# A later due time for one GpSimd clear in the work list of an attention, soft-MoE and MLP kernel

## The chip, the core and the metric

The kernel runs on one core of a Trainium2 chip. The metric is device time in microseconds (us) of one execution, lower is better. The core has five engines that run at the same time and wait for each other through semaphores: TensorE (PE in the profile; its weight loads are PEld), VectorE (DVE), ScalarE (ACT), GpSimd (POOL) and SyncE (SP), which here issues nearly all DMAs.

## The reference

```python
def reference(q, k, v, moe_phi, moe_w1, moe_w2, moe2_w_in, moe2_w_out):
    # attention: B=4, H=8, S=576, D=64, stride 32
    scores = q @ k.T / sqrt(D)
    # heads 0..3: keys of the last 32 positions; heads 4..7: keys at the same position modulo 32
    scores = where(mask, scores, -1e9); attn = softmax(scores); x = attn @ v
    x = x.transpose(0, 2, 1, 3).reshape(2304, 512)
    # soft MoE: 8 experts with 4 slots each
    logits = x @ phi
    slot_in = softmax(logits, axis=0).T @ x
    slot_out[e] = relu(slot_in[e] @ w1[e]) @ w2[e]        # w1: 512x1024, w2: 1024x512, float32
    x = softmax(logits, axis=1) @ slot_out
    # MLP: 512 -> 2048 -> 512 with elu
    h = x @ w_in; g = where(h > 0, h, exp(min(h, 0)) - 1)
    return g @ w_out
```

## The kernel before

The program has three stages. **Attention** (about the first 80 us of the trace) works on 20 units, in the order of the string `ORDER`. A unit marked L is a third of the rows of two heads with the local mask, a unit marked S a quarter of the rows of two heads with the strided mask. The units are numbered here from 0 as `ORDER` has them: 2, 6, 7, 8, 10, 11, 13 and 14 are strided, the others local; units 12 and 15 to 19 are local units of the second pair of heads. A unit goes through these steps: scores on TensorE (L543 local, L562 strided, the latter from a copy of q that GpSimd makes in L551), selection by mask, maximum and subtraction on VectorE (L577 to L605), exponential on ScalarE (L610), sum, reciprocal and transpose on VectorE (L614 to L640; the product with the reciprocal of a strided unit is GpSimd's, L629), a product with the mask on GpSimd for local units (L644, `f_keep`), four copies into a block-diagonal tile (L658 on ScalarE, L660 on GpSimd; "spreads" below), the product with v on TensorE (L671 local, L684 strided), and the move of the result into x by ScalarE (L691 local, L697 strided). The block-diagonal tile `bd` has two halves, which units take in turn, so a unit can spread only when the product of the unit two places ahead in the ring has read its half. Transposes of x (L787, moved out by L799) and the logits (L778) follow the units.

The tiles that hold zeros must be cleared once. Some clears stand in the program text; others (`lv`, `lt`) are nodes of a work list like the steps above. Entry 5 of `lt` is GpSimd's clear of the second half of `bd` (L343), and unit 1 waits for it, as the first that uses that half. Entries 0 to 3 clear a buffer `ex`, two parts of the keys tile `kB` (L304, L305) and a tile `pst`; entry 4 (`late_e0`, L326 to L330) makes a small table `e0`.

The order of every engine's instructions in the attention stage is made by `list_order`, while the program is built: a node is (engine, duration, dependencies, key, function, ring, earliest start). Of the nodes of an engine that could start within `AE` of the earliest one, it takes that with the lowest key, books the planned duration, and goes on. One node's planned start thus moves what is chosen after it, on every engine. On the chip each engine then runs its own list in order.

**The soft MoE** (to about 124 us) takes 8 + 8 weight matrices of 2 MB, which SP loads into regions that attention has finished with; the loads of the first matrices are nodes of the same list (`w_node`), so that SP waits for the unit that used the region last. w1 products are L924, w2 products L1015 and, for the last expert, L1010. Between attention and L924 lies a chain of small steps (L391 to L912). The products on TensorE stand in a fixed order with some filler products in between (`warm`, L314). **The MLP** (the rest) is ordered by a list of its own, which does not contain the attention.

Of the kernel before, what the change touches and what calls it, by code (L numbers as in the profile page):

```python
# [19 lines left out]
def attn_moe_mlp(ctx, tc, q, k, v_l, v_s, phi, w1, w2, w_in, w_out, out):  # L20
# [172 lines left out]
    def small(tag, n, name, bufs, *dims):  # L193
        t = sl_p.tile([128, {"pt": 576, "xt": 768}[tag]], F32, tag=tag, name=name, bufs=bufs)
        t = t[:, 0:n]
        if len(dims) == 2:
            t = t.rearrange("p (a b) -> p a b", b=dims[1])
        elif len(dims) == 3:
            t = t.rearrange("p (a b c) -> p a b c", b=dims[1], c=dims[2])
        return t  # L200
# [56 lines left out]
    with tc.manual_schedule():  # L257
# [80 lines left out]
        def clear(e, t, x):  # L338
            if e == "A":
                return lambda: nc.scalar.activation(out=t[:, x:x + 1024], in_=zero.to_broadcast([128, 1024]), func=AF.Copy)  # L340
            return lambda: nc.gpsimd.memset(t[:, x:x + 1024], 0.0)
# [17 lines left out]
        def load_w(e, second, s, *parts):  # L359
            if (e, second) not in wsl:  # L360
                wsl[e, second] = (w_tile_at(s) if isinstance(s, int) else s)[:, 0:4096]
            t = wsl[e, second]
            for a, b in parts or ((0, 4096),):
                nc.sync.dma_start(out=t[:, a:b], in_=(w2 if second else w1)[e, :, a:b])
# [46 lines left out]
        def emit_acc(t, acc, j0, j1):  # L411
# [7 lines left out]
        anodes, count, apools = [], {}, {  # L419
            "sp": (2, []), "sl": (3, []), "ss": (2, []), "cb": (1, []), "pst": (2, []), "mx": (3, []), "sm": (4, []), "tr": (2, []),  # L420
            "bd": (2, []), "o": (2, []), "qw": (2, []), "t": (3, []), "l": (1, []),
        }
# [6 lines left out]
        def an(eng, dur, deps, key, fn, alloc=None, instr=0):  # L429
            anodes.append((eng, dur, list(deps), key, fn, alloc, 0.0))  # L430
            if instr:
                count[len(anodes) - 1] = instr
            return len(anodes) - 1
# [18 lines left out]
        for x in range(0, WB, 1024):  # L452
            lv[3, x] = an("G", 0.95, [], 14.0 + x / 512, clear("G", v3_sb, x))
        lt = [an("G", d, [], x, f) for d, x, f in zip((0.95, 1.15, 1.15, 0.55, 1.5, 1.8), (12.0, 11.0, 11.1, 13.0, 30.0, 9.5), late)]
        RATE = 2.42
        post = []

        def load_node(kind, p, a, b, after=(), pre=None):
# [4 lines left out]
            key = T[need] - (14 if kind != "v" else 9)  # L463
            dur = 128 * 4 * (b - a) / 1e6 * RATE
            if kind == "v" and p >= 2:
# [27 lines left out]
        def w_node(i, e, s, a, b, after, second=0):  # L493
            post.append((200.0 + i, 128 * 4 * (b - a) / 1e6 * RATE, after, lambda: load_w(e, second, s, (a, b)), None))

# [450 lines left out]
        lt = small("pt", 576, "lt", 2, NSET, 32)  # L946
# [540 lines left out]
```

## Time and profile before

| | before |
|---|---|
| median of 3 runs | 346.62 us (346.04 to 347.05) |
| profiled execution | 346.24 us, of which the trace's span is 344.5 us |
| TensorE busy | 327.6 us, 95% of the span |
| VectorE busy | 262.7 us, 76% |
| ScalarE busy | 250.1 us, 73% |
| GpSimd busy | 62.3 us, 18% |
| DMA | 70.51 MB, mean 205 GB/s |

The shares are means over stages that differ: in the first 150 us the DMA engines are full, in the last 200 us they are nearly idle, and GpSimd works in the attention stage almost alone. A row of a timeline gives the start in us, the length in us, the engine and line, and what it writes and reads; "x" counts instructions that follow each other, and a bracket gives the time for which the engine stood idle before, and what ended it. TensorE's float32 products count as two instructions each.

### The profile page before, as it was taken

The page shows a single profiled execution, that of the slowest core. Times are in us where ns is not written, and L with a number is a line of the kernel's source. Part 1 is how long each engine was busy: PE and PEld are TensorE (multiplying, and loading weights), DVE is VectorE, ACT ScalarE, POOL GpSimd, SP SyncE. Part 2 cuts the span into 40 slices and gives each one's busy share as a digit, 9 for nine tenths or more (in the row PEclk, how much of TensorE's full clock was granted, in tenths as well). Part 3 has the DMA queues.
Part 4 walks back from the last instruction along what each step waited for, and adds up shares of the span by engine and source line. Part 5 has one row for each costly group of instructions (what it writes and reads, how often), then busy time and mean ns, then how long its engine had stood idle before and what let it go on. Part 6 is the DMA issues. An engine that isn't in the chain of part 4 may idle for free.

```text
span 344.5 us, 7046 instructions
## 1 busy us (share of the span) xinstructions
PE 327.6 (95%) x2690; PEld 251.3 (73%) x2690; DVE 262.7 (76%) x586; ACT 250.1 (73%) x498; POOL 62.3 (18%) x106
## 2 busy tenths in 40 slices
PE   4689979999899999999999999999999999999995
PEld 3578866774233345888788888878888888888884
DVE  7899888843713649989999999999975755565862
ACT  9588999985125439999998699668776576657770
POOL 8989525530208300000000000000000000000000
PEclk9699999999999999999999999999999999999999
DMA  7999999999999999693000060000011300110201
GB/s 279 401 416 416 421 417 424 423 409 418 420 431 423 406 416 429 245 434 150 1 0 3 0 243 2 0 0 0 3 62 61 122 2 0 63 61 0 92 33 61
DMA packets 12785, 70.51 MB, mean 205 GB/s; under 512 B 1616, under 2 KB 2640, under 8 KB 8912
## 3 DMA queue, kind: packets, MB, share of 16 engines
q1 hardware_dynamic: 12608, 69.93, 49.9%
q8 instruction: 21, 0.34, 0.4%
q10 hardware_dynamic: 144, 0.13, 0.1%
q14 instruction: 12, 0.10, 0.1%
HBM read 65.34 MB, written 4.72 MB: 203 GB/s over the span
## 4 chain that ended last, share of the span: by engine, by line
PE 75%; DMA 9%; DVE 7%; POOL 4%; ACT 3%; issue 2%; DVEq 0%; SPq 0%; POOLq 0%
PE ops L1362 18%; PE ops L1364 18%; PE ops L1363 18%; PE hps L1300 5%; DMA ex<-in_moe_w_dram 4%; DMA q<-in_moe_w_dram 4%; PE o_ps L671 2%; PE xtps L787 2%; PE s_ps L543 2%; PE ops L1355 1%; ACT bd L658 1%; DVE sc L590 1%; PE mps L1189 1%; PE lg L778 1%; PE so L684 1%
## 5 line engine op out<-in xcount | busy, mean ns | idle before, releaser
L1317 DVE SCALAR_TENSOR_TENSOR g<-hps,g 128x512 f32<-128x512 f32 (+2 forms) x84 | 50.9, 610 | 12.7 <-ACT g L1312 11.7
L1308 ACT ACTIVATE g<-hps 128x512 f32<-128x512 f32 (+2 forms) x84 | 44.8, 534 | 7.9 <-PE hps L1300 7.6
L1312 ACT ACTIVATE g<-g 128x512 f32<-128x512 f32 (+2 forms) x84 | 47.8, 572 | 1.4
L1323 ACT ACTIVATE ghi<-g 128x512 fp32r<-128x512 f32 (+1 forms) x39 | 23.2, 596 | 17.0 <-DVE g L1317 15.0
L1323 ACT ACTIVATE rings<-g 128x512 fp32r<-128x512 f32 (+1 forms) x39 | 22.9, 588 | 17.2 <-DVE g L1317 16.2
L1364 PE MATMUL ops<-w,glo 128*128 128x512 f32 (+1 forms) x87 | 32.8, 377 | 0.0
L1364 PE MATMUL ops<-wh,glo 128*128 128x512 f32 x84 | 31.8, 379 | 0.0
L1300 PE MATMUL hps<-pers 128*128 128x512 f32 (+1 forms) x80 | 29.6, 372 | 0.1
L658 ACT ACTIVATE bd<-tr 32x288 f32<-32x288 f32 (+1 forms) x60 | 28.7, 479 | 1.3
L1362 PE MATMUL ops<-w,ghi 128*128 128x512 f32 (+1 forms) x73 | 27.5, 376 | 0.0
L1363 PE MATMUL ops<-w,ghi 128*128 128x512 f32 (+1 forms) x73 | 27.5, 376 | 0.0
L1362 PE MATMUL ops<-w,rings 128*128 128x512 f32 x72 | 27.3, 379 | 0.0
L1363 PE MATMUL ops<-w,rings 128*128 128x512 f32 x72 | 27.3, 379 | 0.0
L1362 PE MATMUL ops<-wh,ghi 128*128 128x512 f32 x70 | 26.8, 383 | 0.0
L1363 PE MATMUL ops<-wl,ghi 128*128 128x512 f32 x70 | 26.5, 379 | 0.0
L1362 PE MATMUL ops<-wh,rings 128*128 128x512 f32 x68 | 25.8, 379 | 0.0
L1363 PE MATMUL ops<-wl,rings 128*128 128x512 f32 x68 | 25.8, 379 | 0.0
L1364 PE MATMUL ops<-w,rings 128*128 128x512 f32 x58 | 22.0, 379 | 0.0
L1364 PE MATMUL ops<-wh,rings 128*128 128x512 f32 x54 | 20.5, 379 | 0.0
L1300 PEld LDWEIGHTS hps<-pers 128*128 128x128 f32 x80 | 15.0, 189 | 6.7 <-DVE xw L990 1.7
L671 PE MATMUL o_ps<-bd,v 128*64 128x128 f32 x288 | 18.8, 283 | 0.5 <-POOL bd L660 0.2
L1327 DVE TENSOR_TENSOR glo<-g,ghi 128x512 fp32r<-128x512 f32 (+1 forms) x23 | 15.0, 651 | 5.2 <-ACT ghi L1323 5.2
(232 smaller groups left out, 777.2 us busy)
## 6 DMA issues: line engine op xcount, KB each, us to landing
v<-in_moe_w_dram SPq DMA_DIRECT2D x3, 2048.0 KB, 11.8
w<-in_moe_w_out_dram SPq DMA_DIRECT2D x3, 2048.0 KB, 12.3
out_dram<-ob SPq DMA_DIRECT2D x17, 256.0 KB, 2.0
w<-in_moe_w_dram SPq DMA_DIRECT2D x2, 2048.0 KB, 11.3
xw<-in_moe_w_dram SPq DMA_DIRECT2D x4, 1024.0 KB, 11.4
w<-in_moe_w_in_dram SPq DMA_DIRECT2D x2, 2048.0 KB, 11.0
q<-in_q_dram SPq DMA_DIRECT2D x6, 576.0 KB, 8.0
kB<-in_k_dram SPq DMA_DIRECT2D x8, 288.0 KB, 7.8
```

The source lines that it names most:

```text
L543: nc.tensor.matmul(ps[32 * b:32 * b + 32, 2 * j:2 * j + 2], qt[:, c0:c0 + 32], kpair(p, i, b), start=True, stop=True,)
L658: nc.scalar.activation(out=o, in_=i, func=AF.Copy)
L671: nc.tensor.matmul(o[64 * e:64 * e + 64, j, :], v_t[p][:, max(i - 1 + k, 0), e, :], pt[:, 4 * j + 2 * e + k], start=(k == 0), stop=(k == 1),)
L1300: nc.tensor.matmul(pairs(t["ps"]), M4[:, 128 * f:128 * f + 128], turns(cTf[:, t0:t0 + n]), start=True, stop=True)
L1308: nc.scalar.activation(out=t["g"][:, y], in_=t["ps"][:, y], func=AF.Exp)
L1312: return lambda: nc.scalar.activation(out=t["g"][:, y], in_=t["g"][:, y], func=AF.Relu, scale=-1.0, bias=1.0)
L1317: return lambda: nc.vector.scalar_tensor_tensor(out=t["g"][:, y], in0=t["ps"][:, y], scalar=0.0, in1=t["g"][:, y], op0=ALU.max, op1=ALU.su ...
L1323: nc.scalar.activation(out=t["hi"], in_=t["g"], func=AF.Copy)
L1327: nc.vector.tensor_tensor(out=t["lo"], in0=t["g"], in1=t["hi"].bitcast(F32), op=ALU.subtract)
L1362: nc.tensor.matmul(y, t["hi"][:, c], wh, start=(f == f0), stop=False)
L1363: nc.tensor.matmul(y, t["hi"][:, c], wl, start=False, stop=False)
L1364: nc.tensor.matmul(y, t["lo"][:, c], wh, start=False, stop=(f == f1 - 1 and x.stop == 512))
```

## The change

One line is added to the builder of the list. Field 6 of a node is its earliest planned start; the clear of the second half of `bd` (`lt[5]`, key 9.5) gets 12.4 there instead of 0.

```diff
         lt = [an("G", d, [], x, f) for d, x, f in zip((0.95, 1.15, 1.15, 0.55, 1.5, 1.8), (12.0, 11.0, 11.1, 13.0, 30.0, 9.5), late)]
+        anodes[lt[5]] = anodes[lt[5]][:6] + (12.4,)
         RATE = 2.42
```

Lines behind it are numbered one higher in the changed kernel. No instruction is added or removed; the lists of all engines are made anew in the attention stage, and the order of the rest of the program stays (ScalarE, VectorE and TensorE alike).

GpSimd's list at the clears and up to the spreads of units 3 and 4 (tr_384 and tr_437 are these units' transposed scores before, tr_407 and tr_451 in the changed kernel; sm_426 and sm_416 belong to unit 6). Before:

```order
L301 MEMSET ex_107 128x1024
L343 MEMSET bd_126 128x2048
L304 MEMSET kB_102 128x1152
...
L644 TENSOR_TENSOR tr_437<-tr_437,lkeep_86 128x384
L551 COPY ex_107<-q30_103 128x32x18
L629 TENSOR_TENSOR pst_93<-ss2_88,sm_426 128x256
L629 TENSOR_TENSOR pst_93<-ss2_88,sm_426 128x32
L660 COPY bd_126<-tr_384 32x12x32
L660 COPY bd_126<-tr_437 32x12x32
L326 MEMSET negm_63 128x1
L328 MEMSET negm_63 32x1 x2
L330 CAST e0_62<-ident_61 32x128 x4
```

Now:

```order
L341 MEMSET v3_106 128x1024
L343 MEMSET bd_126 128x2048
L645 TENSOR_TENSOR tr_265<-tr_265,lkeep_86 128x384
...
L326 MEMSET negm_63 128x1
L328 MEMSET negm_63 32x1 x2
L330 CAST e0_62<-ident_61 32x128 x4
L645 TENSOR_TENSOR tr_451<-tr_451,lkeep_86 128x384
L552 COPY ex_107<-q30_103 128x32x18
L630 TENSOR_TENSOR pst_93<-ss2_88,sm_416 128x256
L630 TENSOR_TENSOR pst_93<-ss2_88,sm_416 128x32
L661 COPY bd_126<-tr_407 32x12x32
L661 COPY bd_126<-tr_451 32x12x32
```

The clear went from in front of both clears of `kB` to right in front of unit 0's mask product, and the making of `e0` from behind the spreads of units 3 and 4 to in front of unit 4's mask product, unit 6's product and these spreads.

ScalarE's list around unit 6's spreads (tr_528 before, tr_594 now); the `ss2_88` exponentials are those of strided units, the second one shown before and the only one now being unit 8's. Before:

```order
L658 ACTIVATE bd_126<-tr_437 32x12x32 x2
L610 ACTIVATE ls3_87<-ls3_87 128x6x32
L658 ACTIVATE bd_126<-tr_528 32x16x18
L691 ACTIVATE xw_100<-o_ps0_98 128x3x128
L658 ACTIVATE bd_126<-tr_528 32x16x18 x3
L610 ACTIVATE ss2_88<-ss2_88 128x16x18
L691 ACTIVATE xw_100<-o_ps1_99 128x3x128
```

Now:

```order
L659 ACTIVATE bd_126<-tr_407 32x12x32 x2
L659 ACTIVATE bd_126<-tr_451 32x12x32 x2
L611 ACTIVATE ls3_87<-ls3_87 128x6x32
L611 ACTIVATE ss2_88<-ss2_88 128x16x18
L659 ACTIVATE bd_126<-tr_594 32x16x18
L692 ACTIVATE xw_100<-o_ps0_98 128x3x128
L659 ACTIVATE bd_126<-tr_594 32x16x18 x3
```

Unit 8's exponential went from behind to in front of unit 6's four spreads and unit 3's evacuation.

TensorE's list at the last strided product (`so`, unit 14: so_1159 and so_1173 before, so_1189 and so_1203 now). Before:

```order
L543 MATMUL s_ps1_97<-kA_101,q2_104 32x128 x12
L787 MATMUL xtps_1152<-ident_61,xw_100 128x128 x3
L684 MATMUL so_1159<-bd_126,v3_106 64x72 x8
L684 MATMUL so_1173<-bd_126,v3_106 64x72 x8
L671 MATMUL o_ps1_99<-bd_126,v0_83 64x128 x12
```

Now:

```order
L672 MATMUL o_ps1_99<-bd_126,v0_83 64x128 x12
L788 MATMUL xtps_1182<-ident_61,xw_100 128x128 x3
L685 MATMUL so_1189<-bd_126,v3_106 64x72 x8
L685 MATMUL so_1203<-bd_126,v3_106 64x72 x8
```

The product of unit 15 (L671, L672 in the changed kernel) went from behind unit 14's last product to in front of it.

## Rows read from the trace of the kernel before

**Rows 1.** The page's second part: busy tenths in 40 slices, the line of the DMA engines.

```profile
DMA  7999999999999999693000060000011300110201
```

**Rows 2.** The chain that ended last, 80 to 126 us: start, length, what.

```profile
108.64 15.11 DMA q<-in_moe_w_dram
...
123.79 0.43 PE o_ps L1010 x8
```

**Rows 3.** Timeline of TensorE, w2 products of the last experts.

```profile
114.43 1.90 PE L1015 MATMUL o_ps<-v,h1T_b 128*32 128x512 f32 x16
116.26 1.27 PE L314 MATMUL wps<-ident 128*128 128x256 bf16 x10
117.45 2.21 PE L1015 MATMUL o_ps<-kB,h1T_b 128*32 128x512 f32 x16
119.59 1.05 PE L314 MATMUL wps<-ident 128*128 128x256 bf16 x8
120.57 1.64 PE L1015 MATMUL o_ps<-q,ss 128*32 128x512 f32 x8
```

**Rows 4.** Timeline of GpSimd.

```profile
6.11 1.82 POOL L343 MEMSET bd<- 128x2048 f32 x1
...
13.00 1.01 POOL L644 TENSOR_TENSOR tr<-tr,lkeep 128x384 f32<-128x384 f32 x1 [0.28 <-DVE tr L637]
...
28.17 0.09 POOL L326 MEMSET negm<- 128x1 f32 x1
...
30.02 0.50 POOL L660 COPY bd<-tr 32x384 f32<-32x384 f32 x1
```

**Rows 5.** Timeline of ScalarE.

```profile
14.71 2.14 ACT L658 ACTIVATE bd<-tr 32x384 f32<-32x384 f32 x4
...
30.46 0.46 ACT L691 ACTIVATE xw<-o_ps 128x384 f32<-128x384 f32 x1
30.95 1.38 ACT L658 ACTIVATE bd<-tr 32x288 f32<-32x288 f32 x3
32.64 0.45 ACT L610 ACTIVATE ss<-ss 128x288 f32<-128x288 f32 x1 [0.31 <-DVE ss L605]
...
61.06 1.07 ACT L658 ACTIVATE bd<-tr 32x384 f32<-32x384 f32 x2
...
64.33 1.19 ACT L697 ACTIVATE xw<-so 128x288 f32<-128x288 f32 x2
```

**Rows 6.** Stretches: length; PE, PEld, DVE, ACT, POOL busy; granted clock; DMA share; GB/s.

```profile
11.60:18.40 6.80, 5.52 (x78) 4.91 (x80) 6.31 (x22) 3.92 (x9) 6.10 (x10) 0.50 1.02 404
33.00:62.00 29.00, 26.24 (x559) 21.06 (x559) 25.45 (x77) 27.96 (x61) 14.33 (x26) 1.00 1.02 421
```

**Rows 7.** Timeline of VectorE: the same subtraction of two strided units.

```profile
13.28 1.04 DVE L605 TENSOR_TENSOR ss<-sc,mx 128x288 f32<-128x288 f32 x1
...
26.48 0.49 DVE L605 TENSOR_TENSOR ss<-sc,mx 128x288 f32<-128x288 f32 x1
```

**Rows 8.** Timeline of TensorE in the attention stage.

```profile
12.71 2.79 PE L543 MATMUL s_ps<-kA,q 128*32 128x128 f32 x48 [1.68 <-DVE sc L590]
...
62.70 0.55 PE L787 MATMUL xtps<-ident,xw 128*128 128x128 f32 x3
63.17 1.22 PE L684 MATMUL so<-bd,v 128*64 128x72 f32 x32
64.22 1.48 PE L671 MATMUL o_ps<-bd,v 128*64 128x128 f32 x24
```

**Rows 9.** Timeline of SP, two issues that follow each other.

```profile
51.31 1.58 SPq L364 DMA_DIRECT2D q<-in_moe_w_dram  x1
64.46 0.33 SPq L364 DMA_DIRECT2D v<-in_moe_w_dram  x1
```

**Rows 10.** DMA issues, count, KB each, median us to landing.

```profile
out_dram<-ob SPq DMA_DIRECT2D x17, 256.0 KB, 2.0
...
q<-in_moe_w_dram SPq DMA_DIRECT2D x1, 2048.0 KB, 18.4
```

## The prediction

> **What bounds the kernel now.** I read the page's busy tenths first. The DMA engines are full from the second slice to the sixteenth, that is from about 9 us to 138 us [rows 1]; nothing in this stretch can end before the bytes have come. Then the chain that ended last: it goes through the transfer of the last w2 matrix into q, which lands at 108.64 + 15.11 = 123.75 us, and into the products that need it, which end at 123.79 + 0.43 = 124.22 [rows 2]. So the soft MoE ends with its stream of weights, and the MLP behind it has its own order, which the change does not touch. The attention stands in front of all this and is off the chain, as long as it is not too late. How late it may be, I read from TensorE's timeline of the w2 products [rows 3].
>
> TensorE's products run without a gap up to the filler at 116.26. If no transfer made it wait from there, it would need: the filler, 117.45 - 116.26 = 1.19; the sixteen products from kB at the pace of those from v, 116.26 - 114.43 = 1.83 (they took 119.59 - 117.45 = 2.14); the second filler, 120.57 - 119.59 = 0.98; twelve products from q, 12/16 of 1.83 = 1.37; and twice the 0.43 of rows 2 for the last ones, 0.86. That ends at 116.26 + 6.23 = 122.49, against 124.22 in the trace [rows 2, 3]. **TensorE has 1.7 us to spare**: an attention that ends x us later makes the kernel x - 1.7 longer, and one that ends earlier brings nothing.
>
> **The change, part by part.** No work is added; the terms are waits.
>
> *The clear itself.* It takes 1.8 us of GpSimd at 6.11 [rows 4] and now stands in front of unit 0's mask product. Both clears of kB come 1.8 earlier. The mask product ran at 13.00 and comes after the same clears and copies as before with the clear and one clear of v behind them, which is 13.7 by the sum of their lengths: 0.7 late. Its reader, ScalarE, began these spreads at 14.71 [rows 5], when a product of 1.0 from 13.7 is just done: cost 0, hidden by ScalarE's exponential in front. Without that cover it would be 0.7. Unit 1, which waits for the clear, spreads later still. I take 0 here.
>
> *The new lists.* What counts is what ScalarE does around 30 us. Before, it had spread unit 6 (three of four spreads in 1.38 at 30.95, 0.46 each) and evacuated unit 3 (0.46) when it came to unit 8's exponential at 32.64 [rows 5]. Now this exponential stands in front of both, and ScalarE waits in order for VectorE's subtraction of unit 8 (L605). VectorE has as many steps in front of that subtraction as before, so it comes at about the same time, just ahead of 32.64. Behind the exponential there are then four spreads and the evacuation still to do: 5 x 0.46 = 2.3 us. That is a hole in ScalarE, and it cannot be filled: unit 6's transpose stands behind waits for unit 9, and units 3 and 4 spread late because the making of e0 (30.02 - 28.17 = 1.85 of GpSimd [rows 4]) now precedes them.
>
> Another 0.5 comes from VectorE. The subtraction of unit 2 took 1.04 at 13.28 while GpSimd multiplied (13.00 to 14.01), the same instruction without that 0.49 at 26.48 [rows 4, 7]. In the new lists unit 5's mask product is released by the transpose two steps in front of unit 8's subtraction, so the two meet: 0.55 more. At unit 2 the pair no longer meets, but there ScalarE waits for GpSimd anyway. The Trainium skill says in "GPSIMD Engine Reference", section 1, that GpSimd's way into SBUF is shared with VectorE, and that instructions of VectorE with two SBUF inputs contend for it; the trace agrees (1.04 against 0.49). Without such a meeting the sum below would be 0.55 smaller.
>
> So ScalarE is 2.3 + 0.5 = 2.8 us behind at 33 us. Does it catch up? From 33 to 62 us it is busy for 27.96 of 29.00 us [rows 6]: at most 1.04 can be squeezed out. I take a third of it and call the lag L = 2.5. **Bounds:** below, all of it is squeezed and the meeting does not happen, 2.3 - 1.04 = 1.2; above, e0's 1.85 come on top, 4.6.
>
> *From ScalarE's lag to the end of attention.* Unit 15's spreads end at 61.06 + 1.07 = 62.1 before [rows 5]; now at 62.1 + L, and 0.3 for one exponential more in front (under the 0.45 of a strided one). TensorE's product for unit 15 now stands in front of unit 14's last one, so TensorE waits there: 62.4 + L, then this product 1.4 (1.48 less the overlap), a transpose 0.47 and unit 14's product 1.2 [rows 8]. That is 65.5 + L = 68.0, against 63.17 + 1.22 = 64.4: 3.6 later. From there to the end the work is that of before less the product that has already run, 1.4, and with a wait of about 0.7 for the evacuations of unit 14 (0.6 each [rows 5]), which used to run under it. So x = 3.6 - 1.4 + 0.7 = 2.9, in general L + 0.4.
>
> **The sum.** 2.9 - 1.7 = 1.2 us. The profiled execution took 346.24, so it would take 347.4; the median of the runs is 0.4 above it, and with 346.62 the forecast is 347.8. A difference under 0.3%, 1.04 us, cannot be told from no change. With the bounds: L = 1.2 gives x = 1.6 and 346.6; L = 4.6 gives x = 5.0 and 349.9.
>
> **The rivals.**
>
> *No change that can be told.* The lag is under 2.3, so that less than 1.04 comes out behind the 1.7. For it: VectorE and TensorE have gaps of 3.6 and 2.8 us between 33 and 62 [rows 6], so their lateness heals, and if ScalarE's list leaves fewer holes than mine the lag heals too; the stream is full and does not ask. Against it: ScalarE itself has only 1.04 of gaps. Time: 346.6 to 347.6, middle 347.0.
>
> *Faster.* The stream ends earlier. In the first slice the DMA engines are busy 7 tenths [rows 1]; if the loads into kB are held there by GpSimd's clears, which now come 1.8 earlier, the stream starts up to 1.8 earlier and all that follows: 344.8. It decides if SP's queue waits for these clears in the first 12 us. Against it: in the view of SP's waits, the loads into kB are held by earlier loads, not by these clears.
>
> *The queue runs dry.* Unit 14's product also releases the region for the next 2 MB, which SP issued at 64.46 [rows 9]. The transfers in front of it last until 51.31 + 18.4 = 69.7 [rows 9, 10]. A 256 KB store on an empty queue takes 2.0, of which 0.6 is transfer at the 421 GB/s of rows 6, so an issue needs up to 1.4 before bytes flow, and the spare is 69.7 - 1.4 - 64.5 = 3.8. With 3.6 later it just holds. At L = 4.6 the issue is 5.7 late and the stream loses 1.9; TensorE is then 3.3 late by itself, and the longer of the two counts: 349.9. This sets no price of its own unless both add, 351.8, which I give little.
>
> *The clock falls twice.* Between 11.6 and 18.4 us the granted clock is 0.50, the 1.2 GHz level, behind waits of TensorE, and 48 products took 2.79 there [rows 6, 8]. In the new list TensorE waits once more near 17 us, since unit 0's product comes behind a wait for ScalarE. If that holds the low level for another such stretch, its 5.5 us of products take twice the time they need at 2.4 GHz, a loss of 2.8 at most, of which VectorE, busy for 6.31 of 6.80, hides most: say 1 us on x, 348.8. The page "TensorE: Matmul & The Clock Gate" of the Trainium skill, part 1, says that the low clock is the default and that activity releases it; by that rule the extra wait speaks for this rival. Against it: at 12.71 to 18.4 TensorE is busy for most of the time in either order.
>
> **How the numbers follow.** My forecast, slower by more than 1.04 through ScalarE's lag, gets 0.46; the queue and the clock together another 0.08; no change that can be told 0.40; faster 0.06. So slower 0.54, same 0.40, faster 0.06. The range is 346.1 to 349.7: below it lie the faster case and the lowest of no change (the shown runs spread by 0.5 to either side), above it the upper bound and the sums of two rivals. The likeliest case alone spans 347.6 to 349.7.
>
> **What would show it.** Right: ScalarE idle for about 2 us near 31 us in front of unit 8's L610; unit 14's product near 68 in place of 63.17; the chain of small steps behind attention (L391) 2 to 4 us later; L1010 ending near 125.5 without a wait for a DMA in front; DMA engines full in between. Wrong: L1010 still ends at 124.2, with the wait for q still in front of it, which means that the lag was under 1.7; or the last landing in q comes earlier than 123.75, which means that the stream was not the floor; or the DMA tenths show a gap between 65 and 70 us.

## The result: 351.05 us, slower by 1.25%, and the profile after

The changed kernel takes 351.05 us (median of 4 runs, 349.88 to 351.81) against 346.84 us (346.04 to 347.89): 1.0125 of before, 95% interval 1.0106 to 1.0145. The sign was forecast and the mechanism is in the trace, but the time lies 1.35 us over the range. The profiled execution is the lowest of the four, 349.88 us, 3.64 us above that of before; the sums below are made between these two. (By `ORDER` the two units that the prediction calls 14 and 15 at TensorE's end are 13 and 18, and the evacuation that it gives to unit 3 is unit 4's; the instructions are the ones that it means. The mask product in front of which e0 now stands, that of tr_451, is unit 3's and not unit 4's.)

I start where the time is bound. TensorE's timeline in the changed kernel: the end of the strided products, the first w1 product, and the end of the soft MoE:

```profile
66.60 1.53 PE L672 MATMUL o_ps<-bd,v 128*64 128x128 f32 x24 [0.59 <-POOL tr L645]
68.06 0.55 PE L788 MATMUL xtps<-ident,xw 128*128 128x128 f32 x3
68.54 1.22 PE L685 MATMUL so<-bd,v 128*64 128x72 f32 x32
70.80 0.53 PE L779 MATMUL lg<-xw,phi 128*32 128x192 f32 x8 [1.04 <-ACT xw L698]
...
94.38 0.62 PE L925 MATMUL s_ps<-w,siT 128*32 128x512 f32 x2
...
121.45 1.27 PE L314 MATMUL wps<-ident 128*128 128x256 bf16 x10
122.65 1.93 PE L1016 MATMUL o_ps<-kB,h1T_b 128*32 128x512 f32 x16
124.50 1.05 PE L314 MATMUL wps<-ident 128*128 128x256 bf16 x8
125.48 1.48 PE L1016 MATMUL o_ps<-q,ss 128*32 128x512 f32 x10
126.38 0.41 PE L1011 MATMUL o_ps<-q,ss 128*32 128x128 f32 x4
126.79 0.60 PE L1016 MATMUL o_ps<-q,ss 128*32 128x512 f32 x2
127.22 0.61 PE L1011 MATMUL o_ps<-q,ss 128*32 128x128 f32 x12
```

From 121 us no row has a bracket: the wait for q is gone, and TensorE itself is the bound. The end, 127.22 + 0.61 = 127.83, is 3.61 later than 124.22 [rows 2]. The first w1 product came at 89.19 before, so the attention ends x = 5.19 later; 5.19 - 3.61 = 1.58 was absorbed, where the prediction had 1.7.

TensorE before: the logits behind the swapped product, the products in front of the first w1 product, that product, and the wait for q:

```profile
65.63 0.53 PE L778 MATMUL lg<-xw,phi 128*32 128x192 f32 x8
...
84.83 1.05 PE L414 MATMUL s_ps<-xw,ls 128*32 128x512 f32 x4 [0.29 <-DVE dw L883]
85.81 0.38 PE L894 MATMUL tot<-ds,e 128*128 128x1 f32 x2
86.13 1.06 PE L414 MATMUL s_ps<-xw,ls 128*32 128x512 f32 x8
...
89.19 0.62 PE L924 MATMUL s_ps<-w,siT 128*32 128x512 f32 x2
...
122.44 1.05 PE L1015 MATMUL o_ps<-q,ss 128*32 128x512 f32 x4 [0.23 <-DMA q<-in_moe_w_dram]
```

Then ScalarE's timeline of the changed kernel, which has two new holes:

```profile
14.74 0.52 ACT L659 ACTIVATE bd<-tr 32x384 f32<-32x384 f32 x1 [0.41 <-POOL tr L645]
16.80 0.37 ACT L611 ACTIVATE ls<-ls 128x192 f32<-128x192 f32 x1 [1.54 <-DVE ls L606]
17.19 2.15 ACT L659 ACTIVATE bd<-tr 32x384 f32<-32x384 f32 x4
...
33.87 0.45 ACT L611 ACTIVATE ss<-ss 128x288 f32<-128x288 f32 x1 [2.02 <-DVE ss L606]
34.22 0.43 ACT L659 ACTIVATE bd<-tr 32x288 f32<-32x288 f32 x1
...
65.44 1.07 ACT L659 ACTIVATE bd<-tr 32x384 f32<-32x384 f32 x2
```

The second hole is the predicted one: 2.02 us in front of unit 8's exponential, with unit 6's spreads behind it. The first was not predicted: unit 4's exponential (L611 at 16.80) now stands between unit 0's first spread and its other three, and ScalarE waits 1.54 us for VectorE with those three ready. Busy time in two stretches counts what such holes cost (length; PE, PEld, DVE, ACT, POOL busy; clock; DMA share; GB/s), before and after:

```profile
8.00:34.00 26.00, 20.96 (x422) 18.25 (x422) 24.55 (x82) 19.58 (x43) 23.18 (x38) 0.87 1.02 409
8.00:66.00 58.00, 50.20 (x1036) 41.76 (x1036) 52.92 (x169) 50.47 (x110) 37.78 (x62) 0.94 1.02 416
```

```profile
11.60:22.10 10.50, 7.43 (x104) 6.79 (x104) 10.01 (x34) 5.34 (x11) 8.05 (x11) 0.51 1.02 414
...
8.00:34.00 26.00, 19.64 (x382) 17.30 (x384) 23.47 (x79) 16.58 (x35) 21.49 (x36) 0.80 1.02 408
8.00:66.00 58.00, 47.32 (x969) 39.39 (x969) 51.85 (x161) 46.88 (x101) 35.79 (x60) 0.91 1.01 412
```

By 34 us ScalarE has done 19.58 - 16.58 = 3.00 us less work, by 66 us 50.47 - 46.88 = 3.59 less. I call this difference its lag; it never heals. TensorE's end of the attention turns 3.6 into 5.2, by the first rows above: the swapped product (66.60) starts when its spreads end (65.44 + 1.07; its bracket names a mask product on GpSimd that ran from 65.24 to 66.24, but that is another unit's), the last strided product comes behind it, and the logits wait 1.04 us for ScalarE's evacuation; before, the swapped product ran in that gap [rows 8].

The stream is late as well, but in second place. SP's timeline, and the DMA engines from 60 to 130 us in 40 slices of 1.75 us:

```profile
69.83 0.33 SPq L364 DMA_DIRECT2D v<-in_moe_w_dram  x1
```

```profile
DMA  9999818999999999999999999999999999999999
GB/s 431 421 449 421 327 53 234 449 412 384 421 440 328 396 456 431 417 389 426 445 421 407 328 449 431 412 393 440 440 421 431 393 431 400 375 419 389 386 410 412
```

The issue of [rows 9] comes at 69.83 in place of 64.46, 5.4 late where 3.8 was to spare, and the queue runs dry near 70 us: (421 - 327 + 421 - 53 + 421 - 234) / 421 x 1.75 = 2.7 us of stream are lost. Since TensorE is 3.6 late by itself, this adds nothing here: of the two, the longer counts, as the prediction had it.

### The profile page after: what moved, and what is told of

The parts are those of the page before. It is cut to its first block, busy times and chain, and to the rows that moved or that the text cites. A ratio compares the mean times of both kernels' runs of the same rounds, so it can differ in the third digit from the quotient of the medians.

```text
span 348.2 us, 7041 instructions
## 1 busy us (share of the span) xinstructions
PE 327.2 (94%) x2690; PEld 251.9 (72%) x2690; DVE 265.5 (76%) x586; ACT 250.3 (72%) x498; POOL 61.2 (18%) x106
## 4 chain that ended last, share of the span: by engine, by line
PE 81%; ACT 7%; DVE 6%; DMA 3%; issue 2%; POOL 0%; SPq 0%; DVEq 0%; ACTq 0%; POOLq 0%
PE ops L1363 18%; PE ops L1365 17%; PE ops L1364 17%; PE hps L1301 5%; PE s_ps L925 4%; PE o_ps L1016 4%; ACT bd L659 3%; PE o_ps L672 3%; PE xtps L788 2%; ACT xw L698 2%; DMA q<-in_q_dram 2%; PE ops L1356 1%; DVE sc L591 1%; DMA kA<-in_k_dram 1%; PE mps L1190 1%
## 5 line engine op out<-in xcount | busy, mean ns | idle before, releaser
L672 PE MATMUL o_ps<-bd,v 128*64 128x128 f32 x288 | 19.0, 287 | 1.1 <-POOL tr L645 0.6
```

Source lines behind the costliest of these rows:

```text
L672: nc.tensor.matmul(o[64 * e:64 * e + 64, j, :], v_t[p][:, max(i - 1 + k, 0), e, :], pt[:, 4 * j + 2 * e + k], start=(k == 0), stop=(k == 1),)
```

## The experiments

All kernels but one (`late_18`) use one tool. The planner is run twice, once as before and once with the 12.4, and gives each engine two lists, `was` and `now`. A list is edited, and the edited lists are emitted word for word; unedited they are the program before and the changed one. So single moves can be tried without making all lists anew.

```diff
-        order, end = list_order(anodes, apools, AE, ...)
+        was, now = by_engine(plan(0.0)), by_engine(plan(12.4))
+        lists = ...
+        order = replay(lists)
```

Below, A, G, P, V are the lists of ScalarE, GpSimd, TensorE and VectorE, and a number is a node's place in the work list. "Lag" is ScalarE's busy time before less that of the run, 8:34 and 8:66 us, by the view of stretches; x is the first w1 product less 89.19. Lag and x are of one profiled execution; `late_18`, whose attention stage is that of before, shows what that is worth (a lag of 0.3), and `clear_only`, which moves only the clear, differs by 0.5 and 0.8.

| run | time, us | ratio (95%) | lag at 34 / 66 | x |
|---|---|---|---|---|
| changed kernel | 351.05 | 1.0125 (1.0106 to 1.0145) | 3.00 / 3.59 | 5.19 |
| clear_only | 346.75 | 1.0008 (0.9990 to 1.0027) | 0.55 / 0.53 | 0.79 |
| lists_only | 351.68 | 1.0140 (1.0117 to 1.0164) | 3.09 / 5.32 | 7.08 |
| pool_was | 352.34 | 1.0155 (1.0130 to 1.0180) | 2.95 / 4.06 | 6.66 |
| hole1_only | 348.25 | 1.0054 (1.0035 to 1.0074) | 2.08 / 2.37 | 2.86 |
| hole2_only | 349.76 | 1.0090 (1.0059 to 1.0121) | 2.73 / 3.08 | 3.56 |
| unit4_late | 349.19 | 1.0073 (1.0049 to 1.0098) | 3.23 / 3.29 | 3.68 |
| tr_late | 346.90 | 1.0013 (0.9997 to 1.0029) | 2.05 / 2.07 | 2.65 |
| end_swap | 346.45 | 0.9998 (0.9985 to 1.0011) | 1.05 / 1.65 | 1.97 |
| act_lag | 350.91 | 1.0132 (1.0100 to 1.0163) | see text | 4.84 |
| late_18 | 353.39 | 1.0188 (1.0160 to 1.0215) | 0.30 / 0.28 | 7.56 |
| no_holes | 350.78 | 1.0117 (1.0092 to 1.0142) | 2.96 / 4.74 | 6.68 |
| unit4_back_e0 | 351.66 | 1.0137 (1.0105 to 1.0169) | 2.97 / 5.68 | 7.56 |
| repair | 349.91 | 1.0098 (1.0077 to 1.0119) | 2.74 / 3.87 | 5.40 |
| repair_tr | 350.48 | 1.0104 (1.0088 to 1.0119) | 1.18 / 4.34 | 5.91 |
| now34_was | 350.97 | 1.0120 (1.0100 to 1.0139) | 2.89 / 5.17 | 6.04 |
| was34_now | 351.34 | 1.0141 (1.0119 to 1.0162) | 1.90 / 6.84 | 8.16 |
| was20_now | 349.15 | 1.0074 (1.0060 to 1.0087) | 2.54 / 3.16 | 4.44 |
| now50_was | 349.81 | 1.0082 (1.0062 to 1.0101) | 2.99 / 5.17 | 5.52 |

### Is it the clear, or the lists?

```diff
# clear_only: was, and (44 is unit 0's mask product)
+        move(lists['G'], lt[5], before=44)
# lists_only: now, and (lt[1] is the first clear of kB)
+        move(lists['G'], lt[5], before=lt[1])
# pool_was: now, and
+        lists['G'] = list(was['G'])
```

> The lists of all engines are those of the kernel before; only GpSimd's clear of the second half of bd stands where the change puts it, right in front of unit 0's mask product. Theory (the new lists of ScalarE, VectorE and TensorE make the loss, not the clear): the time of before, 346.8 us within 0.3%. Rival (the clear in front of the mask product delays units 0 and 1, and all that follows): most of the 4.2 us, 349 us or more.

> The lists of the changed kernel, with GpSimd's clear back in its old place, in front of both clears of kB. Theory: the loss stays, 350 to 351 us. Rival (the clear): the time of before, 346.8 us.

> GpSimd's whole list is that of before (the clear, and the making of e0 behind the spreads of units 3 and 4); all other engines have the lists of the changed kernel. Theory as it stands after the trace (ScalarE's own list has two holes, 1.54 us at 15 us and 2.02 us at 32 us): 350 us or more, since the holes stay. If the making of e0 in front of those spreads carries its 1.85 us, as the upper bound of the prediction had it, about 349 us.

The clear alone costs nothing that can be told; the lists without it cost all. GpSimd's whole list of before, with e0 behind the spreads, does not help either, so the prediction's upper bound, e0's 1.85 us on top, is not borne out; since a list of before among new ones can make misfits of its own, the run does not price e0 by itself. `clear_only` also tries the slack: its first w1 product is 0.79 late, and the end still waits for q.

```profile
89.98 0.62 PE L975 MATMUL s_ps<-w,siT 128*32 128x512 f32 x2
...
122.47 1.05 PE L1066 MATMUL o_ps<-q,ss 128*32 128x512 f32 x4 [0.23 <-DMA q<-in_moe_w_dram]
```

### What single moves cost in the lists of before

```diff
# hole2_only: was, and unit 8's exponential in front of unit 6's first spread
+        move(lists['A'], 201, before=164)
# hole1_only: was, and unit 4's exponential behind unit 0's first spread
+        move(lists['A'], 116, after=45)
# end_swap: was, and unit 18's product in front of the last strided one
+        move(lists['P'], 462, before=256)
# unit4_late: was, and unit 4's first spread behind unit 6's product with the reciprocal,
# its spreads on ScalarE behind unit 2's evacuation, its product behind unit 11's first scores
+        move(lists['G'], 122, after=162)
+        move(lists['A'], 123, after=93)
+        move(lists['A'], 125, after=123)
+        move(lists['P'], 126, after=282)
# tr_late: was, and the transposes of units 6 and 5 behind unit 9's sum
+        move(lists['V'], 163, after=241)
+        move(lists['V'], 144, after=163)
```

> The lists of before with one move: ScalarE's exponential of unit 8 in front of unit 6's four spreads and the evacuation behind the first, the prediction's main term by itself. By the prediction (hole of 2.3 us, x = 2.7, 1.7 us to spare): 1.0 us over before, 347.6 us. If a lag of ScalarE grows on the way by the 1.1 us that the repeated spreads showed: 2.3 + 1.1 - 1.6 = 1.8 us, 348.4 us. If the hole comes back: 346.6 us.

> The lists of before with one move: ScalarE's exponential of unit 4 in front of unit 0's last three spreads, as the changed kernel has it (1.54 us of idle time there, not in the prediction). If that hole is carried: 1.5 + 1.1 - 1.6 = 1.0 us over before, 347.6 us. If ScalarE, which has gaps of 2 us and more between 17 and 32 us before, catches up: 346.6 us.

> The lists of before with one move: TensorE's product of the early local unit of the second pair in front of the last strided product. The prediction gave the swap 0.4 us of x; the changed kernel shows 1.3 to 1.7 us of x behind ScalarE's lag. Either is under the 1.6 us to spare: 346.6 us, and x itself (the end of the attention) tells: 0.4 or 1.3 to 1.7 us.

> The lists of before on all engines, but for unit 4's two spreads on GpSimd and two on ScalarE and its product on TensorE, which stand as late as the changed kernel has them (product behind unit 8's scores and the first half of unit 11's). Theory C (the ring of two halves of bd: unit 4's slip makes unit 6's spreads, and so ScalarE, late): 349 us or more, with ScalarE about 3 us more idle by 38 us. Rival D (no single step, the whole packages of lists): under 348 us.

> The lists of before, with VectorE's transposes of units 6 and 5 as late as the changed kernel has them (behind unit 9's sum). If one engine's list alone can hold ScalarE up: a hole of about 2 to 3 us in front of unit 6's spreads, and 1.5 to 2.5 us over before, 348 to 349 us. If ScalarE can do without: 346.6 us.

ScalarE in `hole2_only`, and in `hole1_only`:

```profile
33.56 0.44 ACT L610 ACTIVATE ss<-ss 128x288 f32<-128x288 f32 x1 [2.47 <-DVE ss L605]
```

```profile
17.30 0.36 ACT L610 ACTIVATE ls<-ls 128x192 f32<-128x192 f32 x1 [1.26 <-DVE ls L605]
17.69 3.75 ACT L658 ACTIVATE bd<-tr 32x384 f32<-32x384 f32 x7
```

The predicted move makes a hole of 2.47 us (2.3 predicted) and costs 349.76 - 346.48 = 3.3 us, more than either expectation; its runs spread widely (347.71 to 351.44), and the profiled one, 348.51, is 2.3 above that of before, with x = 3.56. So the mechanism is right and x is more than the hole. The unpredicted hole costs 1.8 us by itself. The swap at TensorE's end costs nothing by itself, although it makes the attention 2.0 later than before (1.2 later than `clear_only`): the slack takes all but 0.4 of it, by the profiled execution. `unit4_late` shows that not only ScalarE's own list can open the hole: with unit 4's product late (it runs from 32.40), unit 6's spreads lack their half of bd until 34.01. `tr_late` opens one of 1.76 us, which costs 0.25 us in the median, inside the noise. Its profiled run, 348.33, is one of the higher of a spread from 346.01 to 348.58, and there the hole does show: x is 2.65 and the end 2.1 later. What the faster executions do otherwise no trace shows.

Not all of these prices come through TensorE. In `hole1_only`, `tr_late` and `pool_was` the wait for q is back (q's products start at 124.98, 124.51 and 128.60, behind a DMA), and the end is 2.5, 2.1 and 6.2 us later than before, where x less the slack of 1.58 would be 1.3, 1.1 and 5.1. There the late stream sets the time, so that 1.8 us is not the price of ScalarE's lag alone. In `pool_was` the queue is nearly dry near 70 us, as in the changed kernel; in the other two only shallow dips show, and where the stream loses its time is open.

### Is a lag carried, and what is to spare?

```diff
# act_lag: was, and unit 6's fourth spread nine times
+        spread = anodes[167][4]
+        anodes[167] = anodes[167][:4] + (lambda: [spread() for _ in range(9)],) + anodes[167][5:]
# late_18 (lists of before)
+        for _ in range(18):
+            nc.vector.tensor_copy(out=acc_sb[1][:, 0:192], in_=dl[2])
         emit_dt(2)
```

> The lists of before; ScalarE repeats unit 6's fourth spread eight times near 32 us (the same values), 8 x 0.46 = 3.7 us of pure lag. If a lag of ScalarE is carried to the end (x = 3.7 + 0.4 by the prediction) and TensorE has 1.7 us to spare: 2.4 us over before, 349.0 us; with x = 3.7 + 1.7, as the changed kernel shows it: 350.3 us. If ScalarE catches up on the way: under 348 us.

> The lists of before; VectorE makes 18 more copies of 128x192 (0.26 us apart, 4.7 us in all) in the chain behind attention, in front of the transpose whose reader is TensorE. If TensorE has 1.6 to 1.7 us to spare: 3.0 to 3.1 us over before, 349.7 us. If there is no spare time: 351.3 us. If the stream hides all: 346.6 us.

```profile
31.30 5.16 ACT L658 ACTIVATE bd<-tr 32x288 f32<-32x288 f32 x11
...
94.03 0.62 PE L970 MATMUL s_ps<-w,siT 128*32 128x512 f32 x2
...
126.45 1.05 PE L1061 MATMUL o_ps<-q,ss 128*32 128x512 f32 x4 [0.23 <-DMA q<-in_moe_w_dram]
```

In `act_lag` eight spreads of 5.16 / 11 = 0.47 are 3.75 us of lag, and x is 4.84: the lag is carried whole and grows by 1.1. The time rises by 4.2 us, as much as the change costs. Here the wait for q is back, since its queue ran dry too (two slices at 126 and 253 GB/s near 70 us, two at 218 and 278 near 83): the stream is late on its own account, which is why the loss exceeds 4.84 - 1.58.

In `late_18` the copies took 5.27 us, 0.29 each, and x came out at 7.56, which no expectation had. The rest is TensorE's clock:

```profile
84.84 5.27 DVE L882 COPY acc_sb<-ss 128x192 f32<-128x192 f32 x18 [0.42 <-ACT ss L400]
...
90.45 1.92 PE L414 MATMUL s_ps<-xw,ls 128*32 128x512 f32 x4 [5.46 <-DVE dw L885]
92.30 0.59 PE L896 MATMUL tot<-ds,e 128*128 128x1 f32 x2
92.82 1.93 PE L414 MATMUL s_ps<-xw,ls 128*32 128x512 f32 x8
```

```profile
90.00:95.00 5.00, 4.55 (x16) 1.02 (x16) 1.94 (x9) 0.00 (x0) 0.00 (x0) 0.50 0.77 320
```

TensorE had been idle for 5.46 us, the granted clock is 0.50 (1.2 GHz), and the two groups of products take 1.92 and 1.93 us. In the kernel before they take 1.05 and 1.06, in the rows shown above. That is 1.74 us more, behind 5.27 us of copies and a start that was 0.45 later (78.14 against 77.69 for the first product of L390): 7.46 of the 7.56. So as a trial of the slack its size was off; x is read from its own trace.

### Can the new lists be mended?

```diff
# no_holes: now, and the exponentials of units 4 and 8 behind the last spreads of units 0 and 6
+        move(lists['A'], 116, after=48)
+        move(lists['A'], 201, after=167)
# unit4_back_e0: now, and unit 4's spreads, its product and the making of e0 as before
+        move(lists['G'], 122, after=121)
+        move(lists['G'], 124, after=162)
+        move(lists['G'], lt[4], after=105)
+        move(lists['A'], 123, after=67)
+        move(lists['A'], 125, after=123)
+        move(lists['P'], 126, after=195)
# repair: both of the above, and unit 0's product in front of unit 6's second scores
+        move(lists['P'], 49, before=155)
# repair_tr: repair, and unit 6's transpose in front of unit 9's maximum
+        move(lists['V'], 163, after=237)
```

> The changed kernel with two moves in ScalarE's list: unit 4's exponential behind unit 0's last three spreads, and unit 8's exponential behind unit 6's four spreads. Theory (these two holes are the lag): ScalarE's idle time up to 45 us falls from 11.1 us to about 8, and the time to within 1 us of before, 347 to 348 us. Rival (the holes only show that ScalarE waits for late VectorE or DMA work, and come back elsewhere): 350 us or more.

> The changed kernel with unit 4's four spreads, its product and the making of e0 back in the places that they have before. Theory C: 347 to 348.5 us. Rival D: 350 us or more.

> The changed kernel with every step set back that the traces name by 34 us: unit 4's spreads and product, the making of e0, the exponentials of units 4 and 8 on ScalarE, and unit 0's product on TensorE. If these places are the loss together, each holding the hole open when only the other is mended: 347 to 348.5 us. If the later lists make as much of it: 350 us or more.

> As the repair of all places by 34 us, and VectorE's transpose of unit 6 in the place that it has before (in front of unit 9's maximum), since that transpose ended the hole of 2.20 us that the repair still had at 33 us. If the transpose is the last lock on that hole: ScalarE's idle time by 34 us falls by about 2 us from 9.9, and the time by about 2 us from 349.9 to 348 us. If the hole opens again elsewhere: 349.5 us or more.

The theories that a mended list gives the time back fail here. What ends ScalarE's idle time in front of unit 6's spreads, or of the exponential in their place, in the four kernels in turn:

```profile
34.70 0.45 ACT L658 ACTIVATE bd<-tr 32x288 f32<-32x288 f32 x1 [2.01 <-PE o_ps L671]
```

```profile
36.27 0.45 ACT L610 ACTIVATE ss<-ss 128x288 f32<-128x288 f32 x1 [3.41 <-DVE ss L605]
```

```profile
33.42 0.45 ACT L658 ACTIVATE bd<-tr 32x288 f32<-32x288 f32 x1 [2.20 <-DVE tr L640]
```

```profile
37.98 0.45 ACT L610 ACTIVATE ss<-ss 128x288 f32<-128x288 f32 x1 [2.06 <-DVE ss L605]
```

With the exponentials mended, TensorE's product of unit 4 holds it; with unit 4 mended, the exponential; with both, VectorE's transpose of unit 6; with that mended too, the hole in front of unit 6 is gone (lag 1.18 at 34 us) and one opens four microseconds later in front of the next strided exponential. The last expectation's "opens again elsewhere" is what happened.

The first hole was not removed by any of the four either. In `unit4_back_e0` it stays (1.54 us). In the other three it moves by one exponential, here in `no_holes` and in `repair`:

```profile
20.44 0.37 ACT L610 ACTIVATE ls<-ls 128x192 f32<-128x192 f32 x1 [1.43 <-DVE ls L605]
```

```profile
20.14 0.37 ACT L610 ACTIVATE ls<-ls 128x192 f32<-128x192 f32 x1 [1.89 <-DVE ls L605]
```

This is unit 3's exponential, which the new list of ScalarE has in front of unit 1's last three spreads (they follow at 20.53 in `repair`, 1.58 us for the three). In the kernel before it stands behind them. In the changed kernel it waits only 0.24 us, because the first hole has already cost the time. No run moved it back, so the four attempts do not show that the new lists cannot be mended.

### Where in time does it arise?

```diff
# now34_was (now50_was with 50.0): nodes planned before 34 us as in now, the rest as in was
+        lists = splice(plan(12.4), 34.0, plan(0.0))
# was34_now (was20_now with 20.0): the other way round
+        lists = splice(plan(0.0), 34.0, plan(12.4))
```

> Lists cut in time: all that the planner of the changed kernel starts before 34 us of its own clock stands as in the changed kernel, the rest in the order of before. Theory A (the loss arises by 34 us, where ScalarE stood 3.0 us longer idle than before, and is carried to the end, as the prediction has it): 350 us or more. Theory B (the lateness by 34 us heals, and the later lists make the loss): 347.5 us or less.

> The other half: the order of before up to 34 us of the planner's clock, the order of the changed kernel behind it. Theory A: the time of before, 346.6 us within 0.5%. Theory B: 350 us or more.

> The order of before up to 20 us of the planner's clock (so without the clear's move and without the first hole in ScalarE, at 15 us), the order of the changed kernel behind it. Theory A with the loss in the second hole and around it (as predicted): 349 us or more. If the lists between 12 and 20 us make it: 347.5 us or less.

> The order of the changed kernel up to 50 us of the planner's clock, the order of before behind it, in which TensorE's product of the local unit stands behind the last strided product again. Theory A: as the cut at 34 us, within 0.5 us of it, less what the swap at TensorE's end brings (0.6 to 1.4 us). Theory B: between before and the changed kernel, well above the cut at 34 us.

Each half carries the whole loss, so neither theory of the two cuts at 34 us holds: the lists cannot be cut there into a good and a bad part. The cuts at 20 us (349.15) and at 50 us (349.81) are both lower, and their intervals overlap. The first leaves out the unpredicted first hole; the second keeps it and puts the swap at TensorE's end back, in the size that its expectation gave. The cuts at 34 us have lags of 5.2 and 6.8 at 66 us, more than the changed kernel: a cut makes misfits of its own.

## Why the prediction was wrong, point by point

**What bounds, and the slack: right.** TensorE had 1.58 us to spare (1.7 predicted), then loses one for one: changed kernel 5.19 to 3.61, `late_18` 7.56 to 130.20 - 124.22 = 5.98. This holds where the stream is in time; in four runs the wait for q was back and the loss was larger, and in four others (`hole2_only`, `unit4_late`, `now34_was`, `now50_was`) the end was 0.3 to 0.6 us later than x - 1.58.

**The clear itself at nothing: right** (`clear_only`). What failed beside it is the sentence "I take 0 here" taken for the whole stretch of units 0 and 1: it costs the clear alone, and ScalarE's list had changed there too. Unit 4's exponential in front of three spreads that were ready is 1.54 us of hole; alone it costs 1.8 us.

**The hole in front of unit 8's exponential: right in place, kind and size** (2.3 predicted; 2.02 in the changed kernel, 2.47 alone). In the changed kernel the size is in part luck: ScalarE comes to this exponential 1.5 us later than was assumed, and the subtraction that it waits for is 1.2 us late as well. The 0.5 us of contention did not fall where it was put. VectorE's rows of the changed kernel:

```profile
13.43 0.42 DVE L606 TENSOR_TENSOR ss<-sc,mx 128x288 f32<-128x288 f32 x1
13.76 1.16 DVE L624 TENSOR_TENSOR ls<-ls,sm 128x192 f32<-128x192 f32 x1
...
33.36 0.42 DVE L606 TENSOR_TENSOR ss<-sc,mx 128x288 f32<-128x288 f32 x1
33.69 1.17 DVE L624 TENSOR_TENSOR ls<-ls,sm 128x192 f32<-128x192 f32 x1
```

GpSimd's mask products ran from 13.52 and 33.52. Unit 8's subtraction is just over, and the next instruction of two inputs, unit 9's product, pays: 1.17, where the same instruction without a GpSimd product beside it took 0.35 at 12.44. The subtraction comes at 33.36, not at 32.15 as before, which the prediction assumed, because VectorE is late by then.

**L = 2.5: mis-sized, 3.6.** By chance the lag at 34 us, 3.0, is near the 2.8 of the sum, but half of it is the first hole. From there I let a third of ScalarE's spare 1.04 us be squeezed out; instead the lag grew by another 0.6. `act_lag` shows the same without any new list: of the 3.75 put in, 3.67 stand at 34 us, 4.50 at 66 us (50.47 - 49.72 + 3.75), and x is 4.84.

**x = L + 0.4: mis-sized, L + 1.6.** The product that takes the swap starts at 66.60, where 62.4 + L has 64.9 with the predicted L and 66.0 with the measured one. The 0.6 between is mostly ScalarE: up to this unit's spreads (61.06 before, 65.44 now) it is idle for 3.67 us more than before, and busy for 46.34 - 45.63 = 0.71 more, where one exponential of 0.3 was put. The order behind it was right (66.60 + 3.1 = 69.7, found 69.76). The wait is 1.04 where 0.7 was put, and the product that has already run saves 65.63 - (63.17 + 1.22) = 1.24 where 1.4 was put. So the step that failed is x = 2.9: L is 1.1 short, since the first hole stood at nothing and the lag was taken to shrink where it grew, and what is behind L is 1.2 short. With x = 5.19 the sum is 346.24 + 5.19 - 1.58 = 349.85, and the profiled execution took 349.88.

**The median** lies another 1.2 above that run. Here only one execution's trace exists, and I can't say from which waits the others are longer.

**The rivals.** The queue ran dry, and as predicted did not add. The clock stayed at 0.51 from 11.6 to 22.1 us in place of [rows 6], as that rival said, but the loss does not need it: `repair` has 1.00 in both stretches and is still 1.0098. Nor do the executions of the kernel before follow the clock: three with a mean granted clock under 0.989 have a median of 346.26 us, fourteen with 0.997 or more one of 346.71.

```profile
11.60:18.40 6.80, 5.25 (x87) 4.59 (x86) 6.35 (x22) 3.31 (x7) 5.22 (x7) 1.00 1.02 401
18.40:22.10 3.70, 2.23 (x54) 1.64 (x50) 3.67 (x14) 1.91 (x4) 3.17 (x5) 1.00 1.03 423
```

**What stays open.** Shown is that three single misplaced steps cost 1.8 to 3.3 us each in the lists of before (by medians, in part through the stream), and that ScalarE waits longer in the new lists and TensorE, the bound, comes late behind it. Not shown is a smallest set of moves that gives it back: four attempts each mended the hole that they aimed at or found it held by another engine, all left the first hole in place or moved it by one exponential, and none came under 349.9 us. SP's list differs too, by three pairs of issues that changed places, and no run moved it by itself. VectorE is nearly full to 34 us before (24.55 of 26.00), which fits that any step taken early there makes another late, but no run has taken work off it.

## What to carry to other kernels

When one planned start makes a scheduler redo every list, price the lists and not the moved instruction: walk each in-order engine's list and ask at every row whether something that was ready stands behind something that is not, from the first changed row on and not only at the largest. After a mend, walk it again: here the next exponential held the same hole. An engine that is nearly full for the rest of its stage, as ScalarE was here, can pass a hole on whole (3.75 us came out as 4.84), and the slack behind the stage is subtracted once. Mending one of several orders that hold the same wait shows nothing; only moving it alone in the good version prices it.

## What had not been expected of the hardware

TensorE's granted clock was 1.00 from 76 to 84 us in `late_18`, fell behind an idle stretch of 5.46 us, and stood at 0.50 (1.2 GHz) from 90 to 95 us although TensorE was busy for 4.55 of these 5.00 us. It was 1.00 again from 95 to 100 us. The low level cost 1.74 us of products on the chain. The stretch at 0.50 near the start, on the other hand, was 6.8 us long before, 10.5 in the changed kernel and absent in `repair`, and the times do not follow it.
